# A new order for the first column tile's steps, sums that take their constant in a second summing step, and accumulator steps that wait for one more product

## The chip, the cores and the metric

The kernel runs on one NeuronCore of one Trainium2 chip. The metric is the device time of one execution in microseconds (us). Five engines run side by side, each through its own list of instructions in order: TensorE (PE, with its weight loads shown apart as PEld), VectorE (DVE), ScalarE (ACT), GpSimd (POOL) and SyncE (SP, which here only issues DMAs). They wait for each other by semaphores.

## The reference

```python
def _attn_ref(x, inducing):            # x: 4 x 12416 x 128, inducing: 32 x 128
    scale = 1.0 / np.sqrt(C)
    I = np.broadcast_to(inducing[None], (B, m, C))
    def mab(q, kv):
        s = scale * (q @ kv.transpose(0, 2, 1))
        s = s - s.max(-1, keepdims=True)
        a = np.exp(s)
        a /= a.sum(-1, keepdims=True) + 1e-09
        return a @ kv
    h = mab(I, x)
    return mab(x, h)

def _moe_ref(x, w_gate, w_val, w_out): # x: 49664 x 128, d_ff 1536
    g = x @ w_gate
    silu = g * (1.0 / (1.0 + np.exp(-g)))
    return (silu * (x @ w_val)) @ w_out
```

The output is `_moe_ref` of the flattened `_attn_ref`. Both softmaxes divide by a sum to which 1e-9 is added; these are the constants that the change speaks of.

## The kernel before

The 49664 tokens are four batches of 12416. In each, the first attention gives 32 rows h, and since the second one is a weighted sum of these rows, h is multiplied into the gate and value weights beforehand (`proj_a` to `proj_c` in the first batch). A token then needs only its 32 softmax weights (hi and lo halves, stacked on the partitions in a `stack` tile) against the projected weights `tw`.

**The steady loop.** A batch is cut into 25 column tiles of up to 512 tokens, and d_ff into 12 tiles `t` of 128. One slot is one (column, t). `front` issues two matmuls, gate and value (L679, L680, tile `gv`); `gate` takes silu on ACT (L685); `value` multiplies on DVE (L693, tile `h`, or in place in `gv` for t = 1, 5, 9). `split` rounds `h` to `h_hi` (L701, ACT, DVE for t = 11) and forms `h_lo` (L703, on POOL, or on DVE for t = 1, 5, 9). `back` adds three matmuls into the column's accumulator `o` (L717, L718, L719: `h_hi` by `wo_lo`, `h_hi` by `wo_hi`, `h_lo` by `wo_hi`). A call of `back` is called a product here. Products wait in a list `pend`; about five slots lie between a front and its product. After t = 11 `evac` copies `o` out on DVE (tile `ob`, L726).

**Attention steps in between.** While one batch runs, the steps of the next one, and the later column tiles' own steps, are carried out in the slots that a plan gives them. `sum2` (L455, L456) sums the exponentials of one column group on DVE and adds 1e-9; `rec2` (L459) takes the reciprocal; `norm2` (L463, POOL) multiplies. There are 27 of these. Steps marked `acc` (`s1`, `max_b`, `hacc`, `h_c`, `s2`) take one of the two PSUM buffers of `o` themselves, so they are put off while the next product is t = 11 or t = 0.

**The start.** The first batch's attention, the unpacking of the weights and the whole first column tile (column 0) run in an order written as two strings of tokens, START and SECOND. The weights' bits are loaded as 64-bit words and unpacked in pieces (J0 to J5 for gate and value, o0 to o2 for the output weights): `low` (L178) and `X` (L181) on ACT, `sh` (L184) and `jn` (L187) on DVE, `add` (L190) on POOL. `z0` to `z8` compute the softmax weights of the first column tile's tokens (`z4` holds a sum with 1e-9, L518 and L519), `sM`, `sT`, `m2`, `sb`, `e2`, `sum`, `rec`, `no`, `at`, `ah`, `al` those of the next column group, `pa`, `pk`, `pm`, `pc` or `pb` project piece by piece. `f`, `g`, `m`, `k` are front, gate, value and product of column 0, whose output weights are used unsplit (L715, float32, two passes). `wm:n` issues n transposes of an identity (L633) that compute nothing that is used. The list `ahead` starts with as many waiting products as SECOND leaves, grows by one in six slots up to slot 30 (where an exponential over 1024 columns needs ACT and a change of its table), and then falls back to five.

Of the kernel before, what the change touches and what calls it, by code (L numbers as in the profile page):

```python
# [18 lines left out]
P = 128  # L19
# [11 lines left out]
FC = [4, 16, 16, 16, 15, 15, 15]  # L31
# [6 lines left out]
NT = DFF // P  # L38
# [26 lines left out]
START = """  # L65
lx:0:0:4 lx:0:4:14 lx:1 lx:2 lx:3 lx:4 lx:5 lx:6 ln:4 ln:5 ln:6:0:7 ln:6:7:13 ld:J0:s0 ld:J1:s1 ld:J2:t0 ld:J3:t1 wm:20
tx:0:0 s1:0 tx:0:1:0 tx:0:2 tx:0:3:0 s1:1 tx:1:0 tx:1:1:0 tx:1:2 tx:1:3:0 s1:2 tx:2:0 s1:3 ma:0 tx:2:1:0 tx:2:2 mb:0 tx:2:3:0 e1:0
s1:4 eT:0 tx:3:0 tx:3:1:0 e1:1 tx:3:2 tx:3:3:0 s1:5 eT:1 e1:2 hq:0 s1:6 ma:1 eT:2 e1:3 hq:1 mb:1 eT:3 fs hq:2 ld:o0:x0 ld:J4:x1 ld:J5:x2 su:0 e1:4 hq:3 eT:4 e1:5 hq:4 eT:5 e1:6
eT:6 su:1 hq:5 ha hb hq:6 wm:2 hc
"""  # L70
SECOND = """
X:J0 hd sh:J0 sM:4:20 low:J0 low:J1 jn:J0 sT:4:20 add:J0 ld:o1:s0 X:J1 z0 wm:4 low:J2 z1 z2 m2:4:20 X:J2 sh:J1 z3 low:J3 pa:0 z4 z5 sb:4:20:1 pk:0 pm:0
e2:4:20 jn:J1 sum:1 z6:0 X:J3 z7:0 z8:0 rec:1 z6:1 wm:4 X:o0 sh:J2 z7:1 pc:0 z8:1 jn:J2 sl add:J1 ld:o2:s1 no:1 pa:1 sh:J3 sh:o0 f:0 f:1 jn:o0 pk:1
low:o0 g:0 add:J2 pm:1 jn:J3 m:0 pa:2 pc:1 g:1 pk:2 add:o0 f:2 add:J3 X:J4 at:1 m:1 k:0 X:J5 g:2 low:J4 ah:1:0 sh:J4 sh:J5 f:3 pm:2 pc:2 jn:J4 k:1 g:3
m:2 pa:3 al:1 f:4 pk:3 jn:J5 add:J4 low:J5 g:4 k:2 f:5 m:3 X:o1 pb:3 pa:4 m:4 g:5 sh:o1 m:5 add:J5 pk:4 f:6 jn:o1 g:6 k:3 f:7 low:o1 g:7 pa:5 pb:4 f:8
m:6 f:9 X:o2 sp:1 pk:5 m:7 g:8 pb:5 add:o1 hi:o1 g:9 m:8 k:4 sh:o2 m:9 f:10 hi:o0 f:11 k:5 g:10 m:10 g:11 m:11 jn:o2 low:o2 lo:o1 lo:o0 add:o2
"""
FIRST = {
    12: "sp:2",
# [29 lines left out]
def induced_set_attention_then_swiglu(ctx: ExitStack, tc: tile.TileContext, xt, xn, ind, wgv, wo, out):  # L109
    nc = tc.nc  # L110
# [10 lines left out]
    ps_gv = ctx.enter_context(tc.tile_pool(name="ps_gv", bufs=6, space=bass.MemoryType.PSUM))  # L121
    ps_o = ctx.enter_context(tc.tile_pool(name="ps_o", bufs=2, space=bass.MemoryType.PSUM))
# [75 lines left out]
    def at(u):  # L198

        return AT[u > NG * FC.count(max(FC))]  # L200

    class Batch:
        pass

    def attention(b, one, xn0=None, xt0=None):

        st = Batch()
# [14 lines left out]
        def fblocks(q):  # L222
            return FC0[q], FC0[q] + FC[q]
# [201 lines left out]
        def sl2(b0, b1):  # L425
            return st.s2[:, b0:b1, :]
# [24 lines left out]

        def sum2(q):
            st.sm[q] = att.tile([P, 16], F32, name="sm")
            sm = st.sm[q][:, :FC[q]]
            nc.vector.tensor_reduce(out=sm, in_=sl2(*fblocks(q)), op=ALU.add, axis=AX.X)  # L455
            nc.vector.tensor_scalar(out=sm, in0=sm, scalar1=1e-9, scalar2=None, op0=ALU.add)  # L456

        def rec2(q):
            nc.vector.reciprocal(out=st.sm[q][:, :FC[q]], in_=st.sm[q][:, :FC[q]])  # L459
# [55 lines left out]

        def z4():
            st.zs = att.tile([P, FC[0]], F32, name="zs")
            nc.vector.tensor_reduce(out=st.zs, in_=st.z, op=ALU.add, axis=AX.X)  # L518
            nc.vector.tensor_scalar(out=st.zs, in0=st.zs, scalar1=1e-9, scalar2=None, op0=ALU.add)  # L519
            nc.vector.reciprocal(out=st.zs, in_=st.zs)  # L520

        def z5():
# [94 lines left out]
    with tc.tile_pool(name="xt0", bufs=NCH - NXT) as xt0, tc.tile_pool(name="xn0", bufs=NCH - NXN) as xn0:  # L617
        cur = attention(0, one, xn0, xt0)
        f = cur.f
        bufs = {f"s{i}": s_all[:, 3 * WP * i:3 * WP * i + 3 * WP] for i in range(2)}  # L620
        tw = att.tile([P, 2 * DFF], F32, name="tw")
        bufs |= {f"t{i}": tw[:, 3 * WP * i:3 * WP * i + 3 * WP] for i in range(2)}
        pieces = {}

        def load_piece(p, buf):
            if buf[0] == "x":
                bufs[buf] = xnp.tile([P, max(CH), C], F32, name="xn_sb").rearrange("p a b -> p (a b)")
            pieces[p] = Piece(bufs[buf], p[0], int(p[1]))

        def warm(n):  # L630
            ps = ps_o.tile([P, 512], F32, name="o")
            for i in range(n):
                nc.tensor.transpose(out=ps[:, P * (i % 4):P * (i % 4) + P], in_=ident, identity=ident)  # L633

        def run(token):
            name, *args = token.split(":")
            args = [int(x) if x.isdigit() else x for x in args]
            if name == "ld":
                load_piece(*args)
            elif args and args[0] in pieces:  # L640
# [14 lines left out]
        for token in START.split():
            run(token)
# [48 lines left out]
    acc = {}  # L705
# [24 lines left out]
    pend, wait = [], []  # L730
# [13 lines left out]
    for b in range(B):  # L744
        nxt = attention(b + 1, (one, oneb)[(b + 1) % 2]) if b + 1 < B else None
        if nxt is not None:
            nxt.steps = plan(nxt, PA if b == 0 else PB)
            if b == 0:
                cur.steps.append((nxt.e1, lambda: run(f"e2:52:{NTB}")))
                for q in range(2, NF):  # L750
                    base = NT * (1 + NG * (q - 1) - NST) + 2
                    base = max(base, E0 + 4) if q < 4 else max(base, nxt.e1 + 1)
                    cur.steps += post(cur, q, nc.gpsimd, base)
                cur.steps.sort(key=lambda x: x[0])
        bursts = (nxt.bursts if nxt is not None else set()) | ({E0} if b == 0 else set())
        last_burst = max(bursts, default=0)
        for slot in range(NT if b == 0 else 0, SLOTS):
            c, t = slot // NT, slot % NT
            u = front(cur, b, c, t)
            gate(u)  # L760
            value(u)
            u.cast_dve = t in CAST
            u.last = b == B - 1 and slot == SLOTS - 1
            if wait:
                split(wait[0])
                pend.append(wait.pop(0))
            wait.append(u)
# [59 lines left out]
```

## Time and profile before

| | |
|---|---|
| median of 3 runs | 1486.05 us (1485.43 to 1486.51) |
| the profiled execution | 1486.3 us, of which its trace spans 1484.5 us |
| PE busy | 1464.7 us (99%) |
| ACT busy | 1282.4 us (86%) |
| DVE busy | 1210.5 us (82%) |
| POOL busy | 1206.9 us (81%) |
| granted TensorE clock | 1.0 of full speed over the span |

A matmul's duration in the trace includes a tail that overlaps the next one: a 128x512 matmul is shown with 0.39 us, while a busy PE starts one every 0.23 us. So the small losses of PE are seen in the distance between two starts better than in its idle time. The chain that ended last is followed back from the last instruction.

### The profile page before, as it was taken

How to read it: one execution, taken by the hardware profiler on the slowest of the kernel's cores; microseconds unless marked ns; L12 is line 12 of the kernel's file. 1: busy time of each engine (PE TensorE's matmuls, PEld its weight loads, DVE VectorE, ACT ScalarE, POOL GpSimd, SP SyncE). 2: the span in 40 equal slices, each digit the busy share in tenths (PEclk: the TensorE clock that was granted, in tenths of full speed). 3: DMA queues.
4: the chain of work that ended last, by engine and by line, in shares of the span. 5: the costliest groups of instructions: out<-in, count | busy, mean ns of one | idle time of the engine just before them, and what ended most of it. 6: DMA issues, size and time to landing. Idle time of an engine off the chain costs nothing.

```text
span 1484.5 us, 24938 instructions
## 1 busy us (share of the span) xinstructions
PE 1464.7 (99%) x7451; PEld 1165.1 (78%) x7451; DVE 1210.5 (82%) x2086; ACT 1282.4 (86%) x2386; POOL 1206.9 (81%) x995
## 2 busy tenths in 40 slices
PE   8999999999999999999999999999999999999999
PEld 5476777788887776788887787678888888888887
DVE  6888778878888778788788878878888878878877
ACT  4888888889998887899989888799998998999897
POOL 1688768878898778788898877978889898888887
PEclk9999999999999999999999999999999999999999
DMA  9235332222134233121123424221111111111110
GB/s 359 58 97 198 113 103 81 86 58 58 36 115 155 82 134 109 48 66 36 39 60 117 137 87 147 79 71 47 41 41 35 38 41 44 32 42 38 41 41 21
DMA packets 50822, 119.80 MB, mean 81 GB/s; under 512 B 11392, under 2 KB 28288, under 8 KB 50688
## 3 DMA queue, kind: packets, MB, share of 16 engines
q1 hardware_dynamic: 50688, 118.22, 24.8%
q8 instruction: 59, 0.97, 0.3%
q14 instruction: 75, 0.61, 0.1%
HBM read 62.87 MB, written 25.43 MB: 59 GB/s over the span
## 4 chain that ended last, share of the span: by engine, by line
PE 90%; ACT 3%; DVE 2%; POOL 2%; issue 1%; DMA 1%; SPq 0%; DVEq 0%; POOLq 0%; ACTq 0%
PE o L717 17%; PE o L719 17%; PE gv L679 17%; PE gv L680 17%; PE o L718 17%; PE o L264 2%; POOL h_lo L703 1%; PE o L312 1%; ACT silu L685 1%; DMA xt<-xt 1%; ACT h_hi L701 1%; DVE h L693 1%; PE o L715 1%; PE gv L264 0%; POOL s_all L463 0%
## 5 line engine op out<-in xcount | busy, mean ns | idle before, releaser
L703 POOL TENSOR_TENSOR h_lo<-h,h_hi 128x512 fp32r<-128x512 f32 (+1 forms) x890 | 1108.3, 1269 | 229.5 <-ACT h_hi L701 170.4
L685 ACT ACTIVATE silu<-gv 128x512 f32<-128x512 f32 (+1 forms) x1200 | 704.3, 588 | 119.6 <-PE gv L679 82.7
L693 DVE TENSOR_TENSOR h<-gv,silu 128x512 f32<-128x512 f32 (+1 forms) x891 | 594.9, 669 | 203.4 <-ACT silu L685 146.2
L701 ACT CAST h_hi<-h 128x512 fp32r<-128x512 f32 (+1 forms) x788 | 474.9, 603 | 49.4 <-DVE h L693 42.5
L679 PE MATMUL gv<-stack,tw 128*128 128x512 f32 (+1 forms) x1200 | 467.4, 390 | 0.8 <-DVE h L693 0.5
L717 PE MATMUL o<-h_hi,wo_lo 128*128 128x512 f32 (+1 forms) x1188 | 463.7, 390 | 1.7 <-DVE hn L318 1.7
L680 PE MATMUL gv<-stack,tw 128*128 128x512 f32 (+1 forms) x1200 | 461.9, 385 | 1.2 <-ACT silu L685 0.8
L719 PE MATMUL o<-h_lo,wo_hi 128*128 128x512 f32 (+1 forms) x1188 | 457.9, 385 | 0.6
L718 PE MATMUL o<-h_hi,wo_hi 128*128 128x512 f32 (+1 forms) x1188 | 457.2, 385 | 0.0
L717 PEld LDWEIGHTS o<-h_hi,wo_lo 128*128 128x128 f32 x1188 | 222.9, 188 | 78.7 <-issue 37.5
L679 PEld LDWEIGHTS gv<-stack,tw 128*128 128x128 f32 x1200 | 225.4, 188 | 50.5 <-DVE h L693 2.0
L680 PEld LDWEIGHTS gv<-stack,tw 128*128 128x128 f32 x1200 | 225.0, 187 | 50.6 <-ACT silu L685 6.9
L719 PEld LDWEIGHTS o<-h_lo,wo_hi 128*128 128x128 f32 x1188 | 222.7, 187 | 46.3 <-POOL h_lo L703 5.9
L718 PEld LDWEIGHTS o<-h_hi,wo_hi 128*128 128x128 f32 x1188 | 223.1, 188 | 37.4
L693 DVE TENSOR_TENSOR gv<-gv,silu 128x512 f32<-128x512 f32 (+1 forms) x297 | 201.7, 679 | 45.7 <-ACT silu L685 41.2
L703 DVE TENSOR_TENSOR h_lo<-gv,h_hi 128x512 fp32r<-128x512 f32 (+1 forms) x297 | 197.7, 666 | 1.2 <-ACT h_hi L701 0.3
L701 ACT CAST h_hi<-gv 128x512 fp32r<-128x512 f32 (+1 forms) x294 | 167.5, 570 | 5.1 <-DVE gv L693 3.1
L726 DVE COPY ob<-o 128x512 f32<-128x512 f32 (+1 forms) x100 | 66.4, 664 | 1.4 <-PE o L719 1.4
L701 DVE CAST h_hi<-h 128x512 fp32r<-128x512 f32 (+1 forms) x103 | 47.2, 459 | 0.0
L479 POOL TENSOR_TENSOR a_lo<-aT,a_hi 128x512 fp32r<-128x512 f32 (+2 forms) x27 | 35.3, 1309 | 0.4 <-DVE a_hi L474 0.4
L447 POOL TENSOR_TENSOR s_all<-s_all,mx 128x448 f32<-128x448 f32 (+3 forms) x28 | 26.7, 953 | 1.5 <-DVE mx L443 1.5
L190 POOL TENSOR_TENSOR wgv_sb<-s_all 128x512 int32<-128x512 int32 x2 | 2.6, 1298 | 30.7 <-DVE s_all L187 29.4
(149 smaller groups left out, 508.3 us busy)
## 6 DMA issues: line engine op xcount, KB each, us to landing
xt_sb<-xt SPq DMA_DIRECT2D x32, 896.0 KB, 5.1
xn_sb<-xn SPq DMA_DIRECT2D x18, 896.0 KB, 6.4
out<-ob SPq DMA_DIRECT2D x52, 256.0 KB, 2.0
out<-ob SPq DMA_DIRECT2D x48, 240.0 KB, 2.0
stack<-a_hi SPq DMA_DIRECT2D x96, 64.0 KB, 2.0
stack<-a_lo SPq DMA_DIRECT2D x96, 64.0 KB, 2.0
stack<-a_hi SPq DMA_DIRECT2D x96, 60.0 KB, 2.0
stack<-a_lo SPq DMA_DIRECT2D x96, 60.0 KB, 2.0
```

The source lines that it names most:

```text
L264: nc.tensor.matmul(out=ps[32 * j:32 * j + 32, 32 * (lo - b0):32 * (hi - b0)], lhsT=lhsT, rhs=st.xt[q][:, lo - CH0[q]:hi - CH0[q], j, :], s ...
L479: eng.tensor_sub(out=st.al[q][:, :n], in0=st.at[q][:, :n], in1=st.ah[q][:, :n].bitcast(F32))
L679: nc.tensor.matmul(out=u.g[:, :n], lhsT=st.w[:, wcol(0, t)], rhs=rhs, start=True, stop=True)
L680: nc.tensor.matmul(out=u.v[:, :n], lhsT=st.w[:, wcol(1, t)], rhs=rhs, start=True, stop=True)
L685: nc.scalar.activation(out=u.s[:, :u.n], in_=u.g[:, :u.n], func=AF.Silu)
L693: nc.vector.tensor_mul(out=u.h[:, :n], in0=u.v[:, :n], in1=u.s[:, :n])
L701: (nc.vector.tensor_copy if u.cast_dve else nc.scalar.copy)(out=u.hi[:, :n], in_=u.h[:, :n])
L703: eng.tensor_sub(out=u.lo[:, :n], in0=u.h[:, :n], in1=u.hi[:, :n].bitcast(F32))
L717: nc.tensor.matmul(out=o[:, :n], lhsT=wo_lo[:, ws], rhs=u.hi[:, :n], start=(t == 0), stop=False)
L718: nc.tensor.matmul(out=o[:, :n], lhsT=wo_hi[:, ws], rhs=u.hi[:, :n], start=False, stop=False)
L719: nc.tensor.matmul(out=o[:, :n], lhsT=wo_hi[:, ws], rhs=u.lo[:, :n], start=False, stop=(t == NT - 1))
L726: nc.vector.tensor_copy(out=ob[:, :n], in_=o[:, :n])
```

## The change

Four things are done.

1. START and SECOND are written in another order. One line of each (the rest of the table is moved tokens):

```diff
-s1:4 eT:0 ... s1:5 eT:1 e1:2 hq:0 s1:6 ma:1 eT:2 e1:3 hq:1 mb:1 eT:3 fs hq:2 ...
+s1:4 eT:0 ... s1:5 eT:1 e1:2 hq:0 eT:2 e1:3 s1:6 ma:1 hq:1 mb:1 fs eT:3 hq:2 ...
-X:J0 hd sh:J0 sM:4:20 low:J0 low:J1 jn:J0 sT:4:20 add:J0 ld:o1:s0 X:J1 z0 wm:4 low:J2 z1 z2 m2:4:20 X:J2 ...
+X:J0 hd sh:J0 X:J1 jn:J0 low:J0 sh:J1 X:J2 low:J1 add:J0 ld:o1:s0 jn:J1 z0 z1 sM:4:20 z2 z3 pa:0 sT:4:20 ...
```

The three short `wm` (2, 4 and 4 transposes) are gone and the first one (20) takes a `gv` buffer. For the first column group `sb` and `al` go from POOL to DVE, `ah` from DVE to ACT. Pieces 0 and 4 are projected with `pb` (DVE) and 1, 2, 3, 5 with `pm` and `pc` (PE and ACT); before, 0, 1, 2 had `pm` and `pc`. SECOND holds eight products of column 0, where it held six.

2. The sums.

```diff
+    def total(out, in_):
+
+        pair = pairs[:, :out.shape[1], :]
+        nc.vector.tensor_reduce(out=pair[:, :, 0], in_=in_, op=ALU.add, axis=AX.X)
+        nc.vector.tensor_reduce(out=out, in_=pair, op=ALU.add, axis=AX.X)
 ...
         def sum2(q):
             st.sm[q] = att.tile([P, 16], F32, name="sm")
-            sm = st.sm[q][:, :FC[q]]
-            nc.vector.tensor_reduce(out=sm, in_=sl2(*fblocks(q)), op=ALU.add, axis=AX.X)
-            nc.vector.tensor_scalar(out=sm, in0=sm, scalar1=1e-9, scalar2=None, op0=ALU.add)
+            total(st.sm[q][:, :FC[q]], sl2(*fblocks(q)))
 ...
         def z4():
             st.zs = att.tile([P, FC[0]], F32, name="zs")
-            nc.vector.tensor_reduce(out=st.zs, in_=st.z, op=ALU.add, axis=AX.X)
-            nc.vector.tensor_scalar(out=st.zs, in0=st.zs, scalar1=1e-9, scalar2=None, op0=ALU.add)
+            total(st.zs, st.z)
             nc.vector.reciprocal(out=st.zs, in_=st.zs)
 ...
+    prp = ctx.enter_context(tc.tile_pool(name="prp", bufs=1))
+    pairs = prp.tile([P, 16, 2], F32, name="pairs")
+    nc.gpsimd.memset(pairs, 1e-9)
```

Every second element of `pairs` stays 1e-9; the sum is written beside it, and a second reduction adds the two.

3. The `acc` steps are put off at one product more.

```diff
-                    if getattr(a.steps[0][1], "acc", False) and pend and pend[0].t in (NT - 1, 0):
+                    if getattr(a.steps[0][1], "acc", False) and pend and pend[0].t in (NT - 1, 0, 1):
```

4. The buffer of the transposes and the engine table.

```diff
         def warm(n):
-            ps = ps_o.tile([P, 512], F32, name="o")
+            ps = ps_gv.tile([P, 512], F32, name="gv")
 ...
-            at=f["aT"], ah=lambda q, e=0: f["a_hi"](q, dve_act[e]),
+            at=f["aT"], ah=lambda q, e=0: f["a_hi"](q, (f["same"], nc.scalar.copy)[e]),
```

On POOL, the start's work (in both kernels these are its first large instructions; `wgv_sb` is written by the `add` of J0 to J5 and `xn_sb`, from `xn_sb`, by that of o0; `s_all` by `mx` is `sb`, `s_all` by `sm` is `no`). Before:

```order
L190 TENSOR_TENSOR wgv_sb<-s_all 128x512
L447 TENSOR_TENSOR s_all<-s_all,mx_521 128x512
L190 TENSOR_TENSOR wgv_sb<-s_all 128x512
L463 TENSOR_TENSOR s_all<-s_all,sm 128x512
L190 TENSOR_TENSOR wgv_sb<-tw 128x512
L190 TENSOR_TENSOR xn_sb<-xn_sb 128x512
L190 TENSOR_TENSOR wgv_sb<-tw 128x512
L479 TENSOR_TENSOR a_lo<-aT,a_hi 128x512
```

Now:

```order
L191 TENSOR_TENSOR wgv_sb<-s_all 128x512 x2
L191 TENSOR_TENSOR wgv_sb<-tw 128x512
L191 TENSOR_TENSOR xn_sb<-xn_sb 128x512
L191 TENSOR_TENSOR wgv_sb<-tw 128x512
L468 TENSOR_TENSOR s_all<-s_all,sm 128x512
L191 TENSOR_TENSOR wgv_sb<-xn_sb 128x512 x2
```

The `add` of o0 stands fourth, where it stood sixth; `sb` and `a_lo` have left this engine, and `no` stands behind the `add` of J3.

On DVE, from the scaled rows of h (`hTs`) to the first column tile's normalized weights (`z`). Before:

```order
L380 TENSOR_SCALAR hTs<-gv 128x32
L184 TENSOR_SCALAR s_all<-s_all 128x512
L187 SCALAR_TENSOR_TENSOR s_all<-s_all 128x512
L435 STREAM_TRANSPOSE s_all<-gv 128x512
L506 TENSOR_REDUCE zm<-gv 128x4
L510 TENSOR_TENSOR z<-gv,zm 128x128
L443 TENSOR_REDUCE mx_521<-s_all 128x16
L184 TENSOR_SCALAR s_all<-s_all 128x512
L518 TENSOR_REDUCE zs<-z 128x4
L519 TENSOR_SCALAR zs<-zs 128x4
L520 RECIPROCAL zs<-zs 128x4
L523 TENSOR_TENSOR z<-z,zs 128x128
```

Now:

```order
L387 TENSOR_SCALAR hTs<-gv 128x32
L185 TENSOR_SCALAR s_all<-s_all 128x512
L188 SCALAR_TENSOR_TENSOR s_all<-s_all 128x512
L185 TENSOR_SCALAR s_all<-s_all 128x512
L188 SCALAR_TENSOR_TENSOR s_all<-s_all 128x512
L511 TENSOR_REDUCE zm<-gv 128x4
L515 TENSOR_TENSOR z<-gv,zm 128x128
L442 STREAM_TRANSPOSE s_all<-gv 128x512
L206 TENSOR_REDUCE pairs<-z 128x4
L207 TENSOR_REDUCE zs<-pairs 128x4
L524 RECIPROCAL zs<-zs 128x4
L527 TENSOR_TENSOR z<-z,zs 128x128
```

Two pieces, J0 and J1, are now unpacked ahead of `zm`, the transpose of the next group's scores has moved behind `z`, and the addition of the constant is the second reduction. (In the new list one more reduction, `mx`, stands between the reciprocal and the last row.)

On PE, during the first batch, one step `s1` of the next batch (`o` by `indT`). Before:

```order
L679 MATMUL gv<-stack,tw 128x512
L680 MATMUL gv<-stack,tw 128x512
L264 MATMUL o<-xt_sb,indT 32x448 x4
L717 MATMUL o<-h_hi,wo_lo 128x512
L718 MATMUL o<-h_hi,wo_hi 128x512
L719 MATMUL o<-h_lo,wo_hi 128x512
```

Now:

```order
L686 MATMUL gv<-stack,tw 128x512
L687 MATMUL gv<-stack,tw 128x512
L724 MATMUL o<-h_hi,wo_lo 128x512
L725 MATMUL o<-h_hi,wo_hi 128x512
L726 MATMUL o<-h_lo,wo_hi 128x512
L686 MATMUL gv<-stack,tw 128x512
L687 MATMUL gv<-stack,tw 128x512
L271 MATMUL o<-xt_sb,indT 32x448 x4
```

The step has moved behind one product and one front. Eight steps have moved so: two more `s1`, three `hacc`, two `s2`.

## Rows read from the trace of the kernel before

**Rows 1.** The page: the chain that ended last, by engine.

```profile
PE 90%; ACT 3%; DVE 2%; POOL 2%; issue 1%; DMA 1%; SPq 0%; DVEq 0%; POOLq 0%; ACTq 0%
```

**Rows 2.** Busy time by stretch: length, PE, PEld, DVE, ACT, POOL, clock, DMA.

```profile
28.50:40.00 11.50, 9.08 (x78) 5.01 (x78) 10.21 (x24) 9.93 (x20) 5.24 (x5) 1.00 0.77 283
40.00:50.00 10.00, 7.56 (x20) 3.44 (x20) 9.97 (x13) 8.23 (x15) 6.69 (x6) 1.00 0.13 32
42.00:44.00 2.00, 0.81 (x4) 0.39 (x3) 2.00 (x4) 1.94 (x5) 1.79 (x2) 1.00 0.00 0
50.00:62.00 12.00, 11.24 (x33) 6.04 (x34) 10.99 (x18) 9.66 (x18) 6.81 (x6) 1.00 0.17 41
```

**Rows 3.** Waits of PE from 62 us on: us in total, times, longest.

```profile
PE o L717 <- DVE hn L318: 1.7, 1, 1.7
PE o L264 <- DVE ob L726: 1.5, 3, 0.6
PE o L312 <- DVE ob L726: 1.1, 3, 0.4
```

**Rows 4.** Waits of PE's weight loads, whole span.

```profile
PEld gv L680 <- ACT silu L685: 6.9, 27, 1.0
PEld o L719 <- POOL h_lo L703: 5.9, 13, 0.5
```

**Rows 5.** Timeline behind one sum: start, us, engine, line [idle before].

```profile
1175.25 1.30 POOL L703 TENSOR_TENSOR h_lo<-h,h_hi 128x512 fp32r<-128x512 f32 x1 [0.16 <-ACT h_hi L701]
...
1175.54 1.05 DVE L456 TENSOR_SCALAR sm<-sm 128x16 f32<-128x16 f32 x1
...
1176.50 0.68 DVE L693 TENSOR_TENSOR h<-gv,silu 128x512 f32<-128x512 f32 x1
...
1177.91 1.31 POOL L703 TENSOR_TENSOR h_lo<-h,h_hi 128x512 fp32r<-128x512 f32 x1 [1.36 <-ACT h_hi L701]
...
1181.11 0.39 PE L718 MATMUL o<-h_hi,wo_hi 128*128 128x512 f32 x1
...
1181.54 0.50 PE L719 MATMUL o<-h_lo,wo_hi 128*128 128x512 f32 x1
```

**Rows 6.** Timeline of DVE in the start.

```profile
22.95 0.17 DVE L292 TENSOR_REDUCE negmax<-gv 128x1 f32<-128x12 f32 x1
...
23.60 0.12 DVE L338 TENSOR_TENSOR m<-negmax 128x1 f32<-128x1 f32 x1
...
29.86 0.42 DVE L184 TENSOR_SCALAR s_all<-s_all 128x512 uint32<-128x512 uint32 x1
30.32 0.69 DVE L187 SCALAR_TENSOR_TENSOR s_all<-s_all 128x512 uint32<-128x512 uint32 x1
...
32.12 0.29 DVE L506 TENSOR_REDUCE zm<-gv 128x4 f32<-128x128 f32 x1 [0.26 <-PE gv L502]
...
33.58 0.28 DVE L518 TENSOR_REDUCE zs<-z 128x4 f32<-128x128 f32 x1
33.89 0.70 DVE L519 TENSOR_SCALAR zs<-zs 128x4 f32<-128x4 f32 x1
```

**Rows 7.** Timeline of POOL in the start.

```profile
33.41 1.16 POOL L447 TENSOR_TENSOR s_all<-s_all,mx 128x512 f32<-128x512 f32 x1 [0.85 <-DVE mx L443]
35.87 1.29 POOL L190 TENSOR_TENSOR wgv_sb<-s_all 128x512 int32<-128x512 int32 x1 [1.30 <-ACT tw L181]
...
42.21 1.53 POOL L190 TENSOR_TENSOR xn_sb<-xn_sb 128x512 int32<-128x512 int32 x1 [1.24 <-PE gv L392]
```

**Rows 8.** Timeline of PE in the start: the first front, the first product.

```profile
38.55 0.47 PE L679 MATMUL gv<-stack,tw 128*128 128x512 f32 x1 [0.21 <-DVE stack L540]
...
43.79 1.12 PE L715 MATMUL o<-h_hi,xn_sb 128*128 128x512 f32 x2 [1.19 <-POOL xn_sb L190]
```

**Rows 9.** Timeline around the longest wait: a sum's constant and the matmul behind it.

```profile
210.06 1.09 DVE L456 TENSOR_SCALAR sm<-sm 128x15 f32<-128x15 f32 x1
...
212.11 0.50 PE L717 MATMUL o<-h_hi,wo_lo 128*128 128x512 f32 x1 [1.74 <-DVE hn L318]
```

More of the change, by code (lines that the diff above doesn't have):

```diff
@@ L67 @@
 tx:0:0 s1:0 tx:0:1:0 tx:0:2 tx:0:3:0 s1:1 tx:1:0 tx:1:1:0 tx:1:2 tx:1:3:0 s1:2 tx:2:0 s1:3 ma:0 tx:2:1:0 tx:2:2 mb:0 tx:2:3:0 e1:0
-s1:4 eT:0 tx:3:0 tx:3:1:0 e1:1 tx:3:2 tx:3:3:0 s1:5 eT:1 e1:2 hq:0 s1:6 ma:1 eT:2 e1:3 hq:1 mb:1 eT:3 fs hq:2 ld:o0:x0 ld:J4:x1 ld:J5:x2 su:0 e1:4 hq:3 eT:4 e1:5 hq:4 eT:5 e1:6
-eT:6 su:1 hq:5 ha hb hq:6 wm:2 hc
+s1:4 eT:0 tx:3:0 tx:3:1:0 e1:1 tx:3:2 tx:3:3:0 s1:5 eT:1 e1:2 hq:0 eT:2 e1:3 s1:6 ma:1 hq:1 mb:1 fs eT:3 hq:2 ld:o0:x0 ld:J4:x1 ld:J5:x2 su:0 e1:4 hq:3 eT:4 e1:5 hq:4 eT:5 e1:6
+eT:6 su:1 hq:5 ha hb hq:6 hc
 """
 SECOND = """
[L72 to L76, printed above, removed]
+X:J0 hd sh:J0 X:J1 jn:J0 low:J0 sh:J1 X:J2 low:J1 add:J0 ld:o1:s0 jn:J1 z0 z1 sM:4:20 z2 z3 pa:0 sT:4:20 low:J3 z4 m2:4:20 z5 add:J1 ld:o2:s1 low:J2
+low:o0 X:o0 sh:J2 X:J3 sb:4:20:0 z6:0 z7:0 jn:J2 pk:0 z6:1 z7:1 z8:0 pb:0 pa:1 z8:1 sh:o0 sh:J3 e2:4:20 add:J2 jn:o0 pk:1 f:0 pm:1 sl g:0 pc:1 f:1
+jn:J3 pa:2 f:2 g:1 add:o0 m:0 pk:2 X:J4 sum:1 f:3 pm:2 add:J3 rec:1 m:1 g:2 X:o1 k:0 pa:3 pc:2 g:3 low:J4 sh:J4 m:2 f:4 f:5 jn:J4 k:1 pk:3 sh:o1 g:4
+m:3 no:1:1 pm:3 k:2 at:1 X:J5 sh:J5 pc:3 g:5 low:J5 jn:J5 low:o1 jn:o1 add:J4 pa:4 add:J5 f:6 m:4 pk:4 m:5 g:6 pb:4 k:3 f:7 pa:5 m:6 add:o1 ah:1:1 f:8
+al:1:0 g:7 X:o2 pk:5 sh:o2 g:8 low:o2 k:4 pm:5 f:9 jn:o2 pc:5 k:5 f:10 sp:1 m:7 k:6 m:8 f:11 g:9 add:o2 k:7 m:9 g:10 g:11 m:10 m:11 hi:o0 lo:o0 hi:o1
+lo:o1
 """
```

## The prediction

> **What bounds the kernel now.** I read the page first: PE carries 90% of the chain that ended last [rows 1], at full clock, so the kernel is PE's list of matmuls plus the places where that list stands still. The second view was the busy time by stretch, to see where it does: PE is idle for 11.50 - 9.08 = 2.42, 10.00 - 7.56 = 2.44 and 12.00 - 11.24 = 0.76 us in the three stretches from 28.5 to 62 us [rows 2], 5.6 us in all, while DVE is nearly full. The third was the list of waits from 62 us on: three kinds of full waits, 1.7 + 1.5 + 1.1 us [rows 3], and the weight loads that came late [rows 4]. The fourth was the timeline, around each of these waits and through the start. So the change can win about 5.6 us in the start and about as much again in scattered waits, and nothing from the thousand microseconds in which PE starts a matmul every 0.23 us.
>
> **The sums.** In rows 5 the addition of the constant, 128x16 elements, takes 1.05 us: it starts at 1175.54, while POOL works on an `h_lo` from 1175.25 to 1176.55, and ends when POOL does. In the start it is the same with 128x4 elements: 0.70 us [rows 6], under POOL's 33.41 to 34.57 [rows 7]. The reduction in front of it started at 33.58, under the same POOL instruction, and took 0.28 us for 128x128 elements [rows 6]. So a TENSOR_SCALAR within SBUF waits for POOL here and a TENSOR_REDUCE does not. The second reduction reads 128x32 elements; with the 0.28 us of four times as many as the upper end and 0.12 us (a 128x1 row of rows 6) as the lower I take 0.17 us. Each of the sums then gives DVE back 1.05 - 0.17 = 0.85 us or a little more.
>
> The Trainium skill says the same of the ports (SBUF — State Buffer, Who interferes with whom): VectorE and GpSimd share one port pair that one of them holds for a whole instruction, copies and tensor_scalar can need it, a reduction never, and a VectorE instruction with two SBUF inputs does too. The last clause speaks against a part of this change, since `sb` and `al` are moved to DVE with two SBUF inputs each. By that rule they can wait for an `add` of 1.3 us; both stand where DVE has no front waiting behind it, and the sum is the same with and without.
>
> What is DVE's gain worth to PE? Behind the stalled constant the next `h` starts at 1176.50, POOL has nothing to do for 1.36 us, its `h_lo` comes late, then `norm2` is queued in front of the next one, and L719 starts 0.43 us behind L718 where 0.23 is normal; it is also shown 0.11 us longer than a matmul that did not wait [rows 5]. That is 0.20 + 0.11 = 0.31 us, and the weight load of L719 waits so 13 times [rows 4]. With `h` 0.85 us earlier this `h_lo` ends 0.85 us earlier, 0.65 us ahead of need. 13 x 0.31 = **4.0 us**, all of it gone. Two further places follow a stalled sum in the same way, but there the late `h` holds back `gv` and silu, so that L680 waits; its weight loads wait 6.9 us in 27 places [rows 4], most of them in the start and the bursts, and not all of that can come from sums. Between 0 and 6.9 us I take **1.3 us**, about 0.65 us for each of the two places, twice the size of the others, since two slots are hit. At 210.06 the sum stands ahead of `hn`, for which L717 waits 1.74 us [rows 9]: it gets the 0.85 us back, **0.9 us** with rounding, and the rest of this wait stays (the exponential's burst on ACT makes it).
>
> **The steps put off.** Six steps wait for the copy of `o` (`ob`): 1.5 us in three times and 1.1 us in three [rows 3]. They stand behind the product t = 0 and need the buffer that the column before has just left. One product and one front later, 3 x 0.23 + 2 x 0.23 = 1.15 us, the copy is over, since the longest of the waits is 0.6 us. 2.6 us, and a part of the 0.11 us of a resumed matmul, 0.06 us each: **2.9 us**. Two of the eight steps that move did not wait, and win nothing. What the delay makes late is the next batch's softmax, one slot of a plan that spans 300; I cost it at nothing, covered by that plan's slack; were it gone, a slot is 1.15 us, once for each step.
>
> **The start.** It has four links.
>
> (a) `m` stands at 23.60 behind a transpose; now it follows `negmax`, which ends at 23.12 [rows 6]. Everything to `hTs` is a chain of single waits, so the first unpacking comes at 29.86 - 0.47 = 29.39.
>
> (b) Ahead of `zm` now lie four unpackings, 2 x (0.42 + 0.69) [rows 6], less some 0.08 us of overlap each: `zm` at about 31.5 instead of 32.12. Then the constant costs 0.17 instead of 0.70 us. Against that, the last multiplication (two SBUF inputs) may meet the `add` of J1, which now runs from about 32.4; I lay it at 33.4 to 34.0 with a wait. The first front comes at about 37.1 instead of 38.55 [rows 8].
>
> (c) The first product waited 1.19 us for the `add` of o0 [rows 8], which stood sixth on POOL at 42.21 behind `sb` (33.41, 1.16 us) and `no` [rows 7]. Now it is fourth. Laid one behind the other with the durations of these rows, the `add`s come at 31.1, 32.4, 35.5 and, when DVE has unpacked o0, 38.8; with its 1.29 to 1.53 us the first product can start at about 40.9 instead of 43.79: **2.9 us**.
>
> (d) Behind that point PE has little but work. Of its idle time from 40 to 62 us, 2.44 + 0.76 = 3.2 us [rows 2], about 2.0 lie ahead of the first product and 1.2 behind it; in the new order I find 0.5 left. That wins 0.7, and six resumed matmuls at 0.11 us another 0.6; one more `pm` costs 0.23 us. **1.1 us.** The ten transposes that go cost nothing, since PE waits at their places; their cover gone means only more idle time.
>
> The start is 4.0 us, with the bounds 0 (each lead lost to a new wait) and 5.6 + 1.0 (all idle time gone). One thing is owed later: two products fewer wait when column 0 is left, so two fewer cover the exponential at slot 30, at 3 x 0.23 = 0.69 us each. Between 0 and 1.4 us I take 0, since ACT's gap there is filled from fronts as well.
>
> **The sum.** 4.0 + 1.3 + 0.9 + 2.9 + 4.0 = 13.1 us. The profiled execution, 1486.3 us, becomes 1473.2; it lies 0.25 us above the median of 1486.05, from which the forecast is 1473.0 us.
>
> **The rivals.**
>
> *The sums pay nothing on PE.* POOL has `norm2` and then three `h_lo` in a row, and if that queue alone makes L719 late, DVE's 0.85 us change nothing. For it: the late `h_lo` does stand behind `norm2`. Against it: POOL was idle for 1.36 us just before [rows 5]. Then 4.0 and 1.3 us fall out: 1478.3 us.
>
> *The start's lead is lost.* The unpacking, the projection and the first products share DVE and ACT, which are 10.21 and 9.93 us busy in the 11.50 of the first stretch [rows 2]; a wait that my layout missed can give it back, or the exponential at slot 30. For it: DVE has no slack to hide an error. Against it: POOL's queue is shorter by three instructions ahead of o0. 1477.0 us.
>
> *The change doesn't do what it says.* If the second reduction too waits for POOL (it writes beside its own constants, with a stride), 4.0 + 1.3 + 0.9 us are missing and half a microsecond of the start: 1479.7 us. Against it is the 0.28 us of the first one under POOL.
>
> *The clock falls; slower.* The ten transposes kept PE occupied while it waited from 28 to 36 us. If without them the granted clock falls to 1.2 GHz, every microsecond of matmul costs up to another. To end slower it has to eat the 13.1 us and 3.0 more, that is 16 us of matmuls: from 33 us on rows 2 give about 5.5, 7.6 and then 3 us of 11.24, so the clock would have to stay low beyond 53 us. At 55 us it would be 1486.05 - 13.1 + 17.5 = 1490.5 us. Against it: from 42 to 44 us PE was busy for 0.81 of 2.00 us, with no transposes, and the clock was 1.00 [rows 2]. The Trainium skill (TensorE: Matmul & The Clock Gate, Part 1) says that an idle TensorE is put back to half its clock and gets the full one again only after sustained work, which is the mechanism of this rival; the row does not show it at this load.
>
> **How the numbers follow.** The forecast, all four parts within their bounds, 0.68; sums without pay 0.13; start lost 0.12; the reductions wait 0.03; the clock 0.02; more won than laid out (beyond 1468 us, the other waits of L680) 0.02. The range of 1468 to 1479 us takes in the forecast with its bounds and the second and third case. About 0.2%, 3.0 us, is what a measurement of this kernel can tell from no change. All but the clock lie beyond it on the fast side; two of the losses together leave 3.8 us, three none, so I give 0.94 to faster, 0.04 to no change and 0.02 to slower.
>
> **What will show it.** In the profile of the changed kernel the second reduction should stand with less than 0.25 us in all its 28 places; L719 should no longer wait for POOL's `h_lo` 13 times; L264 and L312 no longer for `ob`; L717 should wait for `hn` about 0.9 us. The first front should start near 37.1 and the first product near 40.9 us, with a clock of 1.00 from 28 to 62. The prediction is wrong if the reductions are long, if L719's waits remain behind short ones, or if PE's idle time from 28.5 to 62 us is still above 4 us.

## The result and the profile after

The changed kernel takes 1472.58 us (median of 4 runs, 1472.31 to 1472.66) against 1485.74 for the kernel before (4 runs, 1485.39 to 1486.51): 13.16 us less, a ratio of 0.991 with a 95% interval of 0.9893 to 0.9928. The forecast was 1473.0. The total came out as forecast, but two of the terms behind it did not: the sums won far more than was laid out for them, the new order far less.

The page of the changed kernel, the chain that ended last, by engine [rows 1]:

```profile
PE 96%; ACT 2%; DMA 1%; DVE 1%; issue 0%; SPq 0%; POOL 0%; DVEq 0%; POOLq 0%
```

PE has gone from 90% to 96% of that chain, and POOL and the issue gaps have left it. The busy time by stretch (columns as in rows 2):

```profile
28.50:40.00 11.50, 8.12 (x69) 4.33 (x69) 10.53 (x25) 10.68 (x21) 5.07 (x4) 1.00 0.77 280
40.00:50.00 10.00, 9.42 (x27) 4.88 (x28) 9.56 (x18) 9.88 (x20) 6.14 (x6) 1.00 0.00 1
50.00:62.00 12.00, 12.00 (x39) 6.60 (x37) 8.86 (x15) 10.35 (x21) 7.20 (x7) 1.00 0.27 67
```

PE's idle time there is 3.38 + 0.58 + 0 = 3.96 us, where it was 5.6. The waits of PE from 57 us on are now of four kinds, and none of them is on `ob` (before there were six kinds, of which rows 3 show the three largest):

```profile
PE o L724 <- DVE hn L325: 1.2, 1, 1.2
PE gv L686 <- ACT silu L692: 0.8, 1, 0.8
PE gv L686 <- DVE h L700: 0.5, 2, 0.3
PE gv L687 <- ACT silu L692: 0.2, 1, 0.2
```

Of the weight loads, L726 (L719 of before) no longer waits for `h_lo`, and L687's line in the list of rows 4 has halved:

```profile
PEld gv L687 <- ACT silu L692: 3.4, 11, 0.7
```

The groups of instructions show what the second reduction costs: 0.18 us, 0.16 for the first column tile, where the constant took 1.05 and 0.70 [rows 5, 6] (0.92 us in the mean of its 27 places).

```profile
L207 DVE TENSOR_REDUCE sm<-pairs 128x16 f32<-128x32 f32 (+2 forms) x27 | 4.9, 183 | 0.9
...
L207 DVE TENSOR_REDUCE zs<-pairs 128x4 f32<-128x8 f32 x1 | 0.2, 161 | 0.0
```

The timeline of the start, by engines: DVE from `negmax` to the last multiplication of `z`, POOL's first additions (the first row is two), PE's first front and first product.

```profile
23.06 0.17 DVE L299 TENSOR_REDUCE negmax<-gv 128x1 f32<-128x12 f32 x1 [0.55 <-PE gv L295]
...
31.25 2.93 POOL L191 TENSOR_TENSOR wgv_sb<-s_all 128x512 int32<-128x512 int32 x2 [29.26 <-ACT s_all L179]
...
33.41 0.65 DVE L450 TENSOR_REDUCE mx<-s_all 128x16 f32<-128x512 f32 x1
...
33.98 0.34 DVE L527 TENSOR_TENSOR z<-z,zs 128x128 f32<-128x128 f32 x1
...
37.70 0.50 PE L686 MATMUL gv<-stack,tw 128*128 128x512 f32 x1 [1.18 <-DVE stack L544]
...
39.15 1.52 POOL L191 TENSOR_TENSOR xn_sb<-xn_sb 128x512 int32<-128x512 int32 x1 [1.86 <-PE gv L687]
...
41.66 0.59 PE L722 MATMUL o<-h_hi,xn_sb 128*128 128x512 f32 x1
```

The first front stands at 37.70 (forecast 37.1) and the first product at 41.66 (forecast 40.9); the multiplication of `z` starts at 33.98, where the forecast had its whole stretch end at 34.0, since the reduction `mx` is queued in front of it. `sb` and `al`, for which the prediction allowed a wait on DVE, take 0.68 us each there, with next to no work of POOL beside them, so no row shows one waiting. Around slot 30 a front's first matmul waits for silu, which L679 of before does nowhere among its full waits:

```profile
81.56 1.06 ACT L457 ACTIVATE s_all<-s_all 128x1024 f32<-128x1024 f32 x1
...
82.64 1.28 ACT L692 ACT_TABLE_LOAD   x1
...
83.93 1.09 ACT L692 ACTIVATE silu<-gv 128x512 f32<-128x512 f32 x2
...
84.58 0.51 PE L686 MATMUL gv<-stack,tw 128*128 128x512 f32 x1 [0.77 <-ACT silu L692]
```

### The profile page after: what moved, and what is told of

Its sections match the earlier page's. It is cut to its first block, busy times and chain, and to the rows that moved or that the text cites. A ratio compares the mean times of both kernels' runs of the same rounds, so it can differ in the third digit from the quotient of the medians.

```text
span 1470.5 us, 24917 instructions
## 1 busy us (share of the span) xinstructions
PE 1456.4 (99%) x7442; PEld 1166.8 (79%) x7442; DVE 1187.9 (81%) x2086; ACT 1287.6 (88%) x2388; POOL 1207.9 (82%) x994
## 4 chain that ended last, share of the span: by engine, by line
PE 96%; ACT 2%; DMA 1%; DVE 1%; issue 0%; SPq 0%; POOL 0%; DVEq 0%; POOLq 0%
PE o L724 19%; PE gv L686 18%; PE o L725 18%; PE gv L687 18%; PE o L726 18%; PE o L271 3%; PE o L319 1%; DMA xt<-xt 1%; PE o L722 0%; PE gv L271 0%; ACT silu L692 0%; PE gv L421 0%; SPq L239 0%; DVE h L700 0%; PE o L372 0%
## 5 line engine op out<-in xcount | busy, mean ns | idle before, releaser
L724 PE MATMUL o<-h_hi,wo_lo 128*128 128x512 f32 (+1 forms) x1188 | 463.5, 390 | 1.2 <-DVE hn L325 1.2
L687 PE MATMUL gv<-stack,tw 128*128 128x512 f32 (+1 forms) x1200 | 461.1, 384 | 0.3 <-ACT silu L692 0.2
L726 PE MATMUL o<-h_lo,wo_hi 128*128 128x512 f32 (+1 forms) x1188 | 456.4, 384 | 0.0
L724 PEld LDWEIGHTS o<-h_hi,wo_lo 128*128 128x128 f32 x1188 | 222.9, 188 | 78.6 <-issue 38.0
L687 PEld LDWEIGHTS gv<-stack,tw 128*128 128x128 f32 x1200 | 224.9, 187 | 46.2 <-ACT silu L692 3.4
L726 PEld LDWEIGHTS o<-h_lo,wo_hi 128*128 128x128 f32 x1188 | 222.6, 187 | 40.5
L725 PEld LDWEIGHTS o<-h_hi,wo_hi 128*128 128x128 f32 x1188 | 223.1, 188 | 37.1
L484 POOL TENSOR_TENSOR a_lo<-aT,a_hi 128x480 fp32r<-128x480 f32 (+2 forms) x26 | 35.0, 1347 | 0.0
```

The source lines that it names most:

```text
L484: eng.tensor_sub(out=st.al[q][:, :n], in0=st.at[q][:, :n], in1=st.ah[q][:, :n].bitcast(F32))
L687: nc.tensor.matmul(out=u.v[:, :n], lhsT=st.w[:, wcol(1, t)], rhs=rhs, start=True, stop=True)
L724: nc.tensor.matmul(out=o[:, :n], lhsT=wo_lo[:, ws], rhs=u.hi[:, :n], start=(t == 0), stop=False)
L725: nc.tensor.matmul(out=o[:, :n], lhsT=wo_hi[:, ws], rhs=u.hi[:, :n], start=False, stop=False)
L726: nc.tensor.matmul(out=o[:, :n], lhsT=wo_hi[:, ws], rhs=u.lo[:, :n], start=False, stop=(t == NT - 1))
```

## The experiments

Twelve runs follow, eleven of other kernels and one of the changed kernel again. Each group of runs has its own executions of the kernel before beside it, so the column of differences is what to compare. "Full clock" counts the executions whose mean granted clock is 1.000.

| run | what is in it | median, us (range) | before | difference | full clock |
|---|---|---|---|---|---|
| the change | all four parts | 1472.58 (1472.31 to 1472.66) | 1485.74 | -13.16 | 1 of 4 |
| e_sums | sums alone | 1475.15 (1474.90 to 1475.38) | 1485.56 | -10.41 | 4 of 5 |
| e_sums_stall | sums, and an addition of 0.0 | 1486.29 (1485.98 to 1487.15) | 1485.56 | +0.73 | 10 of 11 |
| e_acc | put-off alone | 1482.41 (1481.99 to 1483.91) | 1485.56 | -3.15 | 11 of 11 |
| e_order | order alone | 1484.52 (1484.09 to 1485.79) | 1485.56 | -1.04 | 0 of 11 |
| e_no_order | sums and put-off | 1473.09 (1472.72 to 1473.81) | 1485.37 | -12.28 | 4 of 4 |
| e_z4 | the change, old constant in `z4` | 1473.91 (1472.79 to 1474.01) | 1485.37 | -11.46 | 1 of 5 |
| e_six | the change, six products in SECOND | 1471.33 (1471.26 to 1472.02; one more execution took 3729.66 and is left out) | 1485.37 | -14.04 | 2 of 3 |
| e_hn | the change, `hacc` one slot earlier | 1471.99 (1471.43 to 1472.58) | 1485.37 | -13.38 | 2 of 4 |
| e_again | the change once more | 1473.35 (1471.79 to 1473.57) | 1485.41 | -12.06 | 1 of 4 |
| e_warm | the change, short `wm` put back | 1472.28 (1471.62 to 1473.05) | 1485.41 | -13.13 | 5 of 5 |
| e_six_hn | e_six and e_hn | 1470.96 (1470.00 to 1472.46) | 1485.41 | -14.45 | 1 of 4 |
| e_all | e_six, e_hn and e_warm | 1470.39 (1469.87 to 1471.09) | 1485.41 | -15.02 | 4 of 4 |

Several times below a point is "counted from `negmax`". The end of the waits for the first loads differs between executions: `negmax` starts at 22.05 us in one profile here (e_order) and at 23.86 in another (e_acc). What follows it is compared from there.

**The sums alone (e_sums).** The second hunk of the change, in the kernel before.

> The kernel before with the second summing step alone (28 places), old order, old rule for the accumulator steps. Theory (DVE's stalled constant makes h_lo, gv and hn late, and the second reduction is short): 4.0 + 1.3 + 0.9 = 6.2 us gone, the 13 waits of L719 for h_lo with them; about 1479.5 against 1485.7. Rival (POOL's own queue of norm2 and three h_lo makes L719 late): only the 0.9 us at hn, 1484.8, and the 13 waits stay. Rival (the second reduction waits for POOL too): 1485.7.

It won 10.41 us, 4.2 more than expected. Both rivals are out: the reductions are 0.18 us long, and the 13 waits of L719 for `h_lo` are gone from its list. Its full waits of PE, where L270 and L318 are L264 and L312 of rows 3, and L724 is L717:

```profile
PE o L270 <- DVE ob L733: 0.9, 3, 0.3
PE o L724 <- DVE hn L324: 0.8, 1, 0.8
...
PE o L318 <- DVE ob L733: 0.4, 1, 0.4
```

The wait for `hn` is 0.9 us shorter, as expected. But the waits on `ob` have halved too, from 2.6 to 1.3 us, although no step was put off: the copy of `o` is DVE's, and is earlier when DVE is.

**The stall put back (e_sums_stall).** One line behind the second reduction of e_sums:

```diff
         nc.vector.tensor_reduce(out=out, in_=pair, op=ALU.add, axis=AX.X)
+        nc.vector.tensor_scalar(out=out, in0=out, scalar1=0.0, scalar2=None, op0=ALU.add)
```

> The same, with one addition of 0.0 (tensor_scalar, in place, 128x16) behind each second reduction, so that the constant comes by the reduction and the stalled instruction is there again. Theory (what PE paid for was DVE standing still under POOL): the additions take 0.7 to 1.1 us where POOL is at work, and the gain of the run without them is gone, 1485.7 or up to 1 us more for the 0.17 us of the second reductions. Rival (the gain comes from anything else about the two reductions): about 1479.5 stays.

All of the gain is gone, 11.1 us between the two runs, and the waits of the weight load are those of rows 4 again. Its groups, with the second reduction and the added line, and its weight loads:

```profile
L207 DVE TENSOR_SCALAR sm<-sm 128x16 f32<-128x16 f32 (+2 forms) x27 | 23.1, 857 | 0.9
...
L206 DVE TENSOR_REDUCE sm<-pairs 128x16 f32<-128x32 f32 (+2 forms) x27 | 4.9, 182 | 0.9
```

```profile
PEld o L727 <- POOL h_lo L711: 5.9, 13, 0.5
```

So it is DVE's 0.86 us in each of these that PE paid for, and nothing else about the reductions (the 0.73 us by which this run lies above the kernel before are not clear of noise: 0.9998 to 1.0015). The Trainium skill (SBUF — State Buffer, Who interferes with whom) says that a tensor_scalar can need the port pair that GpSimd holds and a reduction never does; the two instructions in this one kernel, 0.86 and 0.18 us side by side, agree.

**The put-off alone (e_acc).** The third hunk, in the kernel before.

> The kernel before with the put-off at t = 1 alone. Theory: the six waits on ob go, 2.6 us and their resumed matmuls 0.06 us each, nothing made late: 2.9 us, 1482.8. Rival (the steps that come later hold up the next batch's softmax): a slot of 1.15 us comes back at some of the eight steps, 1484 to 1486.

3.15 us, and the six waits on `ob` are gone. Nothing came back at the steps that moved.

**The order alone (e_order).** START, SECOND, the buffer and the table.

> The changed kernel with the old sums and the old rule for the accumulator steps, so START, SECOND, the buffer of the transposes and the engine table alone. Theory: 4.0 us less the part that hung on the first column tile's constant (0.70 us again instead of 0.17, so some 0.5 us at the first front, which the first product's wait for o0 may cover): 1482.0 to 1482.3, the lead still there at 108 us, behind the exponential at slot 30. Rival (two fewer waiting products cover that exponential): up to 1.4 us of it given back, 1483.4. Rival (lead lost altogether): 1485.7. If this and the two runs of the other parts add up to the 13.2 us of the whole, the parts don't depend on each other.

Only 1.04 us, and the 95% interval of the ratio, 0.9985 to 1.0002, does not exclude no gain at all: the theory fails, the rival of a lead given back is not enough, and the time lies halfway to the rival of a lead lost altogether. Two things show in its trace. The first column tile's constant, which took 0.70 us before, now stands under two additions of POOL in a row:

```profile
30.95 2.84 POOL L191 TENSOR_TENSOR wgv_sb<-s_all 128x512 int32<-128x512 int32 x2 [29.15 <-ACT s_all L179]
...
32.75 1.08 DVE L520 TENSOR_SCALAR zs<-zs 128x4 f32<-128x4 f32 x1
```

And the granted clock falls (the column behind POOL's):

```profile
28.00:30.00 2.00, 1.72 (x14) 1.35 (x18) 1.25 (x3) 1.31 (x3) 0.00 (x0) 1.00 1.03 410
30.00:32.00 2.00, 1.01 (x16) 0.26 (x8) 1.75 (x6) 2.00 (x5) 1.04 (x1) 0.60 1.03 414
32.00:34.00 2.00, 1.40 (x2) 0.50 (x2) 1.93 (x5) 1.97 (x6) 1.79 (x2) 0.50 1.03 348
```

It is back at 1.00 at 38 us. Counted from `negmax`, the first front of e_order comes 0.6 us later than before, and the first product 0.1 us earlier. All eleven executions have the lower clock, so this run does not show what the order wins alone at full clock.

**The change without its order (e_no_order).** The changed kernel with START, SECOND and the table of before.

> The changed kernel with the order, the buffer of the transposes and the engine table of before: sums and put-off together. The order alone won 1.0 us, the sums alone 10.4, the put-off alone 3.15: 14.6 in sum, against 13.2 for the whole. Theory A (the order is worth its 1.0 us in any company; sums and put-off overlap in the waits on ob, which the sums alone shorten from 2.6 to 1.3 us): 10.4 + 3.15 - 1.3 = 12.2 us, 1473.4. Theory B (the order is worth 2 us once the first column tile's constant is no longer held up): 11.2 us, 1474.5. The put-off that pays in full beside the sums: 13.55, 1472.0.

12.28 us, so theory A: the sums and the put-off overlap by 1.28 us, as much as the sums alone took from the waits on `ob` (1.3). Beside them the order is worth 0.88 us by the first measure of the change and -0.22 by the second (e_again).

**One stalled constant (e_z4).**

```diff
-            total(st.zs, st.z)
+            nc.vector.tensor_reduce(out=st.zs, in_=st.z, op=ALU.add, axis=AX.X)
+            nc.vector.tensor_scalar(out=st.zs, in0=st.zs, scalar1=1e-9, scalar2=None, op0=ALU.add)
```

> The changed kernel with the old addition of the constant in the first column tile's sum alone (one instruction; the other 27 sums keep the second reduction). In the order-alone run this addition took 1.08 us under two additions of POOL, and the first front and the first product stood 1.6 and 2.1 us later, counted from negmax, than in the changed kernel. Theory (in the new order this one stall is what holds up the start): the same 1.6 and 2.1 us again, and 1.5 to 2.0 us at the end, 1474.1 to 1474.6. Rival (the two microseconds are lost to other waits further on anyway): within 0.5 us of the changed kernel, 1472.5 to 1473.0.

1.7 us less won than by the change in its first measure and 0.6 less than in its second, so the medians do not decide. At full clock there is one execution here, 1472.79, and the change has one in each measure, 1472.31 and 1471.79: 0.5 to 1.0 us for this one instruction (1.09 us in the profile), from single executions, where e_warm's at full clock spread by 1.4 us. The 1.5 to 2.0 us that were expected are not confirmed, and the size stays open.

The expectation had put down to the constant what is in the main the clock's. Counted from `negmax`, the first front and the first product stand at 15.53 and 20.69 us in e_z4, and at 15.63 and 20.46 in e_again, which has the low clock too but not the old constant; only the changed kernel's profile at full clock has 14.64 and 18.60.

**Six products in SECOND (e_six).** `k:6` and `k:7` are taken out of SECOND and are done later, by the loop.

> The changed kernel with the last two products taken out of SECOND, so that six stand in it as before and two more products wait for the exponential at slot 30. Counted by products, 1.35 us of the changed kernel's lead went there. Theory (two products cover 2 x 0.69 us of the wait, and PE has other work in their old place): the new wait of 0.93 us for silu and its 0.26 us go, up to 1.3 us won, 1471.2 to 1471.7. Rival (PE waits in SECOND's last part for what these products covered): no gain, 1472.5 to 1473.0.

0.9 us against the change's first measure and 2.0 against its second, by the differences to before, and PE's wait of 0.8 us for silu is gone from the list. What happened at slot 30 is seen in the starts of the 13th and the 21st product that is not column 0's, first in the kernel before, then in the changed kernel, then in e_six (timelines of PE):

```profile
83.05 0.39 PE L717 MATMUL o<-h_hi,wo_lo 128*128 128x512 f32 x1
...
92.83 0.39 PE L717 MATMUL o<-h_hi,wo_lo 128*128 128x512 f32 x1
```

```profile
78.89 0.39 PE L724 MATMUL o<-h_hi,wo_lo 128*128 128x512 f32 x1
...
90.04 0.40 PE L724 MATMUL o<-h_hi,wo_lo 128*128 128x512 f32 x1
```

```profile
79.95 0.39 PE L724 MATMUL o<-h_hi,wo_lo 128*128 128x512 f32 x1
...
89.73 0.40 PE L724 MATMUL o<-h_hi,wo_lo 128*128 128x512 f32 x1
```

Between them lie 9.78 us before, 11.15 in the changed kernel and 9.78 in e_six. The changed kernel gives back 1.37 us of its lead at the exponential, and two more waiting products take that back.

**The accumulations one slot earlier (e_hn).** `HA=(2, 2, 2)` for `(3, 3, 3)` in the first plan `PA`.

> The changed kernel with the three accumulations of h of the first plan one slot earlier (HA=(2, 2, 2) for (3, 3, 3)), so that the copy hn stands on DVE ahead of the sum and of the next value. Theory (the rest of that wait is the copy's place in DVE's queue): the wait of 1.21 us of L724 for hn goes, 1471.2 to 1471.5. Rival (the accumulation waits for the transposes, and only stands in PE's way earlier): no gain or a loss of up to 1 us.

The wait for `hn` is gone; by the medians 0.2 us are won over the change's first measure and 1.3 over its second. At full clock it takes 1471.43 and 1471.52, at 0.998 to 0.999 it takes 1472.45 and 1472.58: the clock's part, 1.0 us, is as large as what was sought, so the size stays open here.

**The clock (e_again, e_warm).** The changed kernel again, and the changed kernel with this:

```diff
-... hq:5 ha hb hq:6 hc
+... hq:5 ha hb hq:6 wm:2 hc
-... jn:J1 z0 z1 sM:4:20 ... z6:1 z7:1 ...
+... jn:J1 z0 wm:4 z1 sM:4:20 ... z6:1 wm:4 z7:1 ...
```

> The changed kernel itself, as the measure for the three runs beside it, and for its clock: three of its four executions so far show a mean granted clock of 0.997 or 0.998, one 1.000. Theory (without the three short groups of transposes the clock falls in the start, in most executions but not in all): again most below 1.000, these 0.3 to 1.1 us slower than those at 1.000; about 1472.5.

> The changed kernel with the three short groups of transposes (2, 4, 4) put back at the same steps, in a gv buffer. Theory (the clock's fall to 0.5 between 30 and 38 us comes with PE's missing work there, and costs about 1 us): the clock is 1.00 in all stretches and executions, 1471.4 to 1471.8. Rival (the transposes have no part in it, or stand in PE's way): clock below 1.00 in most executions again, 1472.5 or more.

e_again by stretch, then e_warm:

```profile
28.00:30.00 2.00, 1.63 (x14) 1.40 (x18) 1.32 (x4) 1.59 (x4) 0.00 (x0) 1.00 1.04 420
30.00:32.00 2.00, 1.18 (x16) 0.28 (x11) 1.86 (x5) 2.00 (x5) 1.21 (x1) 0.64 1.02 410
32.00:34.00 2.00, 1.57 (x2) 0.50 (x2) 1.93 (x7) 1.97 (x5) 1.63 (x2) 0.50 0.99 348
34.00:36.00 2.00, 2.00 (x33) 1.38 (x32) 1.33 (x3) 1.47 (x4) 0.54 (x1) 0.50 0.92 340
36.00:38.00 2.00, 2.00 (x11) 0.67 (x4) 1.88 (x4) 1.36 (x4) 0.75 (x1) 0.66 0.51 205
```

```profile
30.00:32.00 2.00, 2.00 (x26) 1.26 (x25) 1.93 (x5) 2.00 (x4) 0.92 (x1) 1.00 1.03 412
32.00:34.00 2.00, 1.21 (x6) 0.30 (x2) 1.91 (x7) 2.00 (x5) 2.00 (x2) 1.00 1.09 383
```

e_again came out 0.85 us above its expectation, and its executions at the low clock 1.5 to 1.8 us above the one at full clock, where 0.3 to 1.1 were expected. Without the transposes the clock is at 1.2 GHz for several microseconds of the start, in three executions of four (by their mean clock; the stretches are those of the one profile), and these take 1473.33 to 1473.57 us against 1471.79 at full clock. With them all five executions are at 1.000, and the median is 1.07 us below that of e_again beside it, though not as low as expected (1471.4 to 1471.8); the full-clock executions still spread by 1.4 us. That the transposes hold the clock is shown: of all executions of the new order, 8 of 35 are at full clock without them and 9 of 9 with them (e_all included). What this is worth is not fixed: against the change's first measure, e_warm's 13.13 us are no gain over 13.16, and the change's own two executions at full clock, 1472.31 and 1471.79, lie in e_warm's range.

**Both repairs, and all three (e_six_hn, e_all).**

> The changed kernel with six products in SECOND and the three accumulations of h one slot earlier. Alone these brought 0.9 and 0.6 us by medians, at mixed clocks. Theory (two waits at different places, 84 and 206 us): both gains add up, 1470.8 to 1471.2 at mixed clocks. Rival (the wait at 206 us is refilled by what was won before): 1471.5.

> The same with the three groups of transposes put back. Theory: the clock stays at 1.00, and the gains of the three edits add up: 0.9 + 0.6 + 0.7 to 1.0 us below the changed kernel, 1470.0 to 1470.3, faster than both kernels. Rival (six products and the transposes win the same microsecond): 1470.8 to 1471.2.

e_six_hn came out within its expectation; only two kinds of full waits are left of the four:

```profile
PE gv L686 <- DVE h L700: 0.5, 2, 0.3
PE gv L687 <- ACT silu L692: 0.2, 1, 0.2
```

e_all is the fastest kernel of the study: 1470.39 us, 0.1 above its expectation and below its rival, 15.02 below the kernel before (ratio 0.9899, 0.9886 to 0.9913) and 2.96 below the changed kernel beside it (1.86 by the differences to before, against the change's first measure).

## Why the total was right and two of its terms were not

That the sum of 13.1 us stands beside 13.16 measured is luck: the sums won 4.2 us more than was laid out, the put-off beside them 1.0 less, and the order beside both of them 3.1 less (4.2 by e_again).

**The sums: right where a wait was followed, too small in all.** The step was "4.0 + 1.3 + 0.9". Measured alone they are 10.4. In the profiles of before and of e_sums, by the starts of the same matmuls, the three terms came true: the 13 late `h_lo`, 4.1 us (forecast 4.0); the two places where the late `h` holds back L680, 0.7 us each, so 1.4 (1.3); `hn`, 0.9 (0.9). One of the two places in the kernel before, where L680 starts 0.50 us behind L679, and 0.23 in e_sums:

```profile
452.32 0.40 PE L679 MATMUL gv<-stack,tw 128*128 128x512 f32 x1
...
452.82 0.50 PE L680 MATMUL gv<-stack,tw 128*128 128x512 f32 x1
```

The other 4.0 us hang on stalled sums too, and were not laid out for them: the waits on `ob`, 1.3 (credited to the put-off); the first column tile's constant, 0.9 at the first front counted from `negmax` (15.60 to 14.70, laid in the start); between the 21st and the 37th product, where two sums follow the exponential of slot 30, 24.2 us became 23.2, so 1.0; the rest, some 0.8, are small waits. The third of these stands in the list of full waits of before, below the three that rows 3 show, and in e_sums it is 0.2 us:

```profile
PE gv L680 <- ACT silu L685: 0.8, 2, 0.6
```

What failed was not a duration but the search for who waits: only the waits named in rows 3, 4 and 9 were followed back, and those on `ob` not to a sum. An early DVE also copies `o` out earlier and fills a burst's gap earlier.

**The put-off: right.** 2.9 forecast, 3.15 alone. Beside the sums it adds 1.9, since they had halved these waits already: the two terms are not independent, and the sum counted them as if they were.

**The start: won as laid out at full clock, then a third of it given back, and more where the clock fell.** The step was "4.0 us, with the bounds 0 ... and 5.6 + 1.0". The order alone won 1.0, and beside the sums nothing that these medians can fix (-0.2 to 0.9). Counted from `negmax`, the 13th product of the three pairs above stands at 60.1 us before and at 55.8 in the changed kernel, with as many fronts done (62): a lead of 4.3 us. At the 21st it is 2.9, and 0.9 of either is the sums', which have it in the old order (e_sums). What is left to the order at full clock is 2.0 us. In e_again, at the low clock, the leads are 2.4 and 1.0 (`negmax` at 22.20), so the order's part is 0.1:

```profile
79.93 0.39 PE L724 MATMUL o<-h_hi,wo_lo 128*128 128x512 f32 x1
...
91.08 0.39 PE L724 MATMUL o<-h_hi,wo_lo 128*128 128x512 f32 x1
```

So the two things that failed are the debt at slot 30, 1.37 us where "between 0 and 1.4 us I take 0" (the reason given, that the gap is filled from fronts, is refuted by e_six), and the clock. Link by link: (a) is right: counted from `negmax`, `hTs` comes 0.42 us earlier (forecast 0.47). (b) has the first front's gain of 0.9 us, but that is the sums' (e_sums has it in the old order, at 14.70 us from `negmax`; the changed kernel has 14.64). (c) holds at full clock only: 18.60 us from `negmax` to the first product, 20.84 before [rows 6, 8], 19.94 in e_sums; so 1.3 of these 2.2 us are the order's, against the 2.9 that were laid out. In e_again, where the clock fell, it is 20.46, and the order's part is lost. (d) won more than the 1.1 us laid out: from the first to the 13th product it is 37.2 us, where it was 39.3.

**The clock: the rival came true in small.** "The clock falls" was priced as a fall that lasts to 55 us, with a chance of 0.02. It falls in most executions of the change, but comes back at 38 us, and costs 0.2 to 1.8 us (between the change's own executions in its two measures; some 0.7 and 1.0 in e_six and e_hn), which can't turn the sign. The argument against it, a stretch with 0.81 us busy of 2.00 at full clock [rows 2], was about one place and one execution. The profile taken of the changed kernel is the one of its four executions at 1.000, so its page alone, with 1.00 in all three stretches from 28.5 to 62 us as the forecast had it, hides this.

**The signs that were named.** The reductions are short in all 28 places, L726 and `ob` wait no more: right. The wait for `hn` is 1.2 instead of 0.9 us; it is 0.8 in e_sums and 0.9 in e_no_order, so the new order leaves it 0.3 to 0.4 longer, and why was not found. The first front and the first product came 0.6 and 0.8 us later than named, and the clock of 1.00 was there in one execution of four. PE's idle time of 3.96 us lies just under the limit of 4 that was set.

## What to carry to other kernels

An instruction that stalls on its engine is worth removing for everything queued behind it, not only for the waits that name it: put the stall back alone, as e_sums_stall does, and the whole price is read off (here 11.1 us of PE's time for 23.1 us of DVE's). Terms that shorten the same wait don't add; run each alone and both together. Before useless matmuls are taken out of a start, look at the granted clock of several executions, not of one profile, and count the waiting work that must cover the next gap.

## What the hardware showed beyond expectation

The same program falls to the low clock in some executions and not in others: one of four at full clock in both measures of the change, none of eleven in e_order, all of five with ten transposes of 128x128 put back (and of four in e_all), and 44 of the 45 executions of the kernel before that ran beside these. The Trainium skill (TensorE: Matmul & The Clock Gate, Part 1) says that how many matmuls of one kernel run at the low clock at its start differs between runs; these executions, 0.997 to 1.000, show such a difference for a fall some 30 us into a kernel, which that sentence does not speak of. The transposes compute nothing that is used, and PE has the time for them: counted from `negmax`, the first front stands at 14.62 us with them (e_warm) and at 14.64 without them at full clock. e_warm's stretch from 30 to 32 us is 2.00 of 2.00 us busy, where the change has 1.78 (in its one profile at full clock) and e_again 1.18.
